# Load order, implied waits, idle matmuls, two copies and score groups: a change to the start of a fused attention and MLP kernel

## The chip, the cores and the metric

The kernel runs on one core of one Trainium2 chip. The metric is the device time of one execution in microseconds (us). Most executions of one kernel lie within about 1 us of each other, but not all, so each kernel is run several times; the span of a profile is some 1.8 us shorter than the time of the same execution, because it counts from the first to the last recorded instruction.

PE is the matmul engine and PEld its weight loads; DVE, ACT (ScalarE), POOL (GpSimd) and SP (SyncE) are the others. A DMA "lands" when its data is there.

## The reference

Attention with a window of 32 positions to each side, for 8 batches and 8 heads of 576 positions and 64 dimensions, and then an MLP with a squared ReLU over all 4608 tokens. Everything enters and leaves as 32-bit floats; the kernel computes in bf16 on PE.

```python
scores = (1 / np.sqrt(64)) * q @ k.transpose(0, 1, 3, 2)           # 8 x 8 x 576 x 576
mask = np.abs(pos[:, None] - pos[None, :]) <= 32
attn = softmax(np.where(mask, scores, -1e9))
x = (attn @ v).transpose(0, 2, 1, 3).reshape(4608, 512)
h = x @ w_in                                                       # 512 x 2048
r = np.maximum(h, 0.0)
out = (r * r) @ w_out                                              # 2048 x 512
```

## The kernel before

The program is written as a list of operations. Each has an engine, what it reads and writes, a planned duration and, for a DMA, planned figures of its queue. A list scheduler orders them: it runs a model forward and backward several times and keeps the order that does best over random repetitions of the model. So a change of one constant can reorder work anywhere.

The early loads go to GpSimd's queue in a written order. `w10` is the first quarter of `w_in`'s columns, `v04` the fifth and last V piece of batch 0:

```python
SIZES = (3,) * 9 + (4,) * 9        # groups of score steps of 64 tokens from batch 1 on
ORDER = ("k01 q01 v00 v01 v02 k03 q03 v03 k04 q04 w10 v04 w11 w12 w13 k05 q05 k10 q10 v10 k11 q11 v11 "
         "w20 w21 w22 w23 k12 q12 v12 k13 q13 v13 k14 q14 v14").split()
```

After scheduling, gaps in PE's plan up to the first MLP tile get idle matmuls, which multiply zeros so that PE's clock stays up:

```python
def fill(self, out):
    at = 1200                                              # ns of the plan
    for op in sorted((o for o in out if o.eng == "PE"), key=lambda o: o.start):
        gap = min(op.start, WARM, self.first.start) - at
        one = 107 if at < COLD else 54
        for k in range(int((gap - 60) * (DENSE if at < COLD else SPARSE) // one)
                       + (EXTRA if op is self.first else 0)):
            ...                                            # one idle matmul of 128 columns
        at = max(at, op.start + op.dur)
```

Last, the waits are written. An engine that has already waited for a value of a semaphore doesn't wait for it again, but what the other engine had itself waited for isn't known:

```python
for s, v in need.items():
    if waited.get((op.eng, s), 0) >= v:
        continue
    waited[(op.eng, s)] = v
    e.wait_ge(sems[s] if s in sems else dsems[s], v)
```

The MLP begins with small tiles of 128 tokens (`mm1_small`, the first of which is "the first MLP tile" below), goes over to 256 and then to 512 tokens. A small tile needs the transposed attention output `xt` and a quarter of `w_in`:

```python
def mm1_small(self, T, g, q, key):                         # cut
    def f(e):
        for d in range(4 * q, 4 * q + 4):
            for ft in range(4):
                mm = e.matmul(ht[:, 128 * (d % 4):...], self.W1[:, ft, 128 * d:128 * d + 128],
                              self.XT[:, ft, t0:t0 + 128], start=(ft == 0), stop=(ft == 3))
        return mm
    first = self.p.rec("PE", f, reads=[("xt", 8 * T + 2 * g), ("xt", 8 * T + 2 * g + 1), ("w1", q)], ...)
```

From step 18 on, `xt` is made by transposing DMAs on SP; before that PE transposes `xr`, the attention output as it comes, and ScalarE copies the result.

The softmax here doesn't subtract the row's maximum and nothing guards it: scores larger than these inputs give would overflow.

## Time and profile before

| | before |
|---|---|
| time, median of the first 3 runs | 300.18 us (299.93 to 300.94) |
| span of the profile | 298.4 us |
| PE busy | 293.1 us, 98% |
| first MLP tile starts | 18.21 us |
| last matmul ends | 296.10 us |

The prediction below shows the lines that it reads. Two more views help to follow it. The page's list of costly groups (line, engine, operation, what it writes and reads, partitions x elements, count, then busy time and mean ns of one, then idle time before) says where PE's time goes, and the list of DMA queues (packets, MB, share of 16 engines' span) how full the loading queue is:

```profile
q0 software_dynamic: 113120, 17.90, 89.8%
...
L919 PE MATMUL outp<-w,gt 128*128 128x512 bf16 x560 | 134.5, 379 | 0.0
...
L867 PE MATMUL ht<-xt,w 128*128 128x512 bf16 x384 | 93.7, 379 | 0.3 <-issue 0.3
```

The two big matmul groups have next to no idle time before them, and the queue that loads inputs and weights is occupied for 90% of the span. The second view is PE's timeline at the start (start us, duration us, what, count). It shows whether the clock is up:

```profile
2.77 2.13 PE L416 MATMUL outp<-zz 128*128 128x128 bf16 x18
...
7.91 1.09 PE L495 MATMUL ht<-oe,pf 128*128 128x128 f32 x8
```

Eighteen idle matmuls of 128 columns take 2.13 us, start to start about 107 ns: cold. From 5.25 us on the same kind takes 56 ns: warm. Eight of the 14 traces also hold records of the granted clock, which `prof` prints only as means; that of before goes up at 5.03 us.

### The profile page before, as it was taken

The numbers are of one execution on the slowest core, as the hardware profiler recorded it, in microseconds if no ns is written. First come the engines' busy times: TensorE is split into PE (matmuls) and PEld (weight loads), VectorE is DVE, ScalarE is ACT, GpSimd is POOL, SyncE is SP. The second block draws the span as 40 slices with busy tenths as digits, with TensorE's granted clock in tenths as the row PEclk, the third lists the DMA queues.
The fourth block names the chain that finished last, engine by engine and source line by source line (L and its number), as shares of the span: only waits on it lengthen the run. The fifth ranks groups of instructions, "written<-read, shape, count | busy, mean of one in ns | idle before, by whom it ended". The sixth has DMA issues, their size and how long they took to land.

```text
span 298.4 us, 7058 instructions
## 1 busy us (share of the span) xinstructions
PE 293.1 (98%) x2789; PEld 172.0 (58%) x2789; DVE 175.7 (59%) x428; ACT 160.5 (54%) x261; POOL 105.2 (35%) x131
## 2 busy tenths in 40 slices
PE   7899999999999999999999999999999999999996
PEld 7799855867668754544444545544445544444445
DVE  5864755674979966866386666773827682322200
ACT  3466543656657654763555656636645565444411
POOL 8999841332425434351254353313520000000000
PEclk9999999999999999999999999999999999999999
DMA  9999999999999999999499999999992230000022
GB/s 153 166 202 170 206 174 194 174 162 165 187 176 131 133 156 149 159 131 187 63 138 153 173 139 171 117 140 148 126 174 81 64 82 9 35 35 35 36 88 90
DMA packets 166817, 39.34 MB, mean 132 GB/s; under 512 B 157824, under 2 KB 162304, under 8 KB 166784
## 3 DMA queue, kind: packets, MB, share of 16 engines
q0 software_dynamic: 113120, 17.90, 89.8%
q1 hardware_dynamic: 46512, 11.15, 25.2%
q10 hardware_dynamic: 7152, 9.83, 10.1%
q8 instruction: 22, 0.36, 0.5%
q14 instruction: 11, 0.09, 0.1%
HBM read 36.70 MB, written 9.44 MB: 155 GB/s over the span
## 4 chain that ended last, share of the span: by engine, by line
PE 95%; DMA 2%; DVE 2%; issue 0%; POOL 0%; POOLq 0%
PE outp L919 41%; PE ht L867 28%; PE ht L849 7%; PE ht L826 7%; PE sc L703 3%; PE sc L647 3%; DMA qraw<-in_q_dram 2%; PE sc L495 1%; DVE vd L547 1%; PE outp L416 1%; PE sc L895 1%; PE outp L895 1%; DVE xr L791 1%; PE ht L495 0%; PE sc L751 0%; PE outp L807 0%
## 5 line engine op out<-in xcount | busy, mean ns | idle before, releaser
L919 PE MATMUL outp<-w,gt 128*128 128x512 bf16 x560 | 134.5, 379 | 0.0
L882 DVE TENSOR_TENSOR gt<-rt 128x512 bf16<-128x512 bf16 x144 | 59.5, 420 | 62.2 <-ACT rt L873 53.6
L867 PE MATMUL ht<-xt,w 128*128 128x512 bf16 x384 | 93.7, 379 | 0.3 <-issue 0.3
L919 PEld LDWEIGHTS outp<-w,gt 128*128 128x128 bf16 x560 | 52.9, 98 | 58.9
L873 ACT ACTIVATE rt<-ht 128x512 bf16<-128x512 f32 x96 | 57.4, 598 | 51.4 <-PE ht L867 48.9
L867 PEld LDWEIGHTS ht<-xt,w 128*128 128x128 bf16 x384 | 36.3, 98 | 41.9 <-issue 0.4
L469 POOL DMA_DIRECT2D qraw<-in_q_dram x39 | 33.6, 863 | 57.4 <-PE ht L867 20.6
L469 POOL DMA_DIRECT2D kraw<-in_k_dram x39 | 33.6, 860 | 35.1 <-PE ht L867 17.2
L535 POOL DMA_DIRECT2D vx<-in_v_dram x40 | 34.6, 866 | 21.3 <-PE ht L867 13.3
L684 DVE TENSOR_TENSOR pt<-e,mask 128x512 bf16<-128x512 bf16 (+1 forms) x63 | 29.9, 508 | 19.9 <-ACT e L668 19.1
L926 ACT ACTIVATE oe<-outp 128x512 f32<-128x512 f32 x35 | 20.9, 597 | 35.0 <-PE outp L919 34.9
L668 ACT ACTIVATE e<-sc 128x1024 bf16<-128x1024 f32 (+1 forms) x36 | 31.8, 917 | 6.4 <-PE sc L647 6.3
L727 DVE TENSOR_TENSOR xr<-pf,rs 128x512 bf16<-128x512 f32 (+1 forms) x42 | 27.5, 682 | 0.4
L826 PE MATMUL ht<-xt,w 128*128 128x128 bf16 x384 | 23.8, 219 | 0.0
L849 PE MATMUL ht<-xt,w 128*128 128x256 bf16 x192 | 23.3, 273 | 0.0
L826 PEld LDWEIGHTS ht<-xt,w 128*128 128x128 bf16 x384 | 21.7, 98 | 0.3
L720 DVE COPY pf<-sc 128x520 f32<-128x520 f32 x21 | 14.6, 697 | 8.8 <-PE sc L703 8.6
L849 PEld LDWEIGHTS ht<-xt,w 128*128 128x128 bf16 x192 | 18.0, 98 | 3.1
L717 ACT ACTIVATE pf<-sc 128x520 f32<-128x520 f32 x21 | 12.6, 602 | 13.0 <-PE sc L703 11.4
L834 ACT ACTIVATE rt<-ht 128x512 bf16<-128x512 f32 x24 | 14.2, 599 | 9.1 <-PE ht L826 8.8
L855 ACT ACTIVATE rt<-ht 128x512 bf16<-128x512 f32 x24 | 14.3, 600 | 6.0 <-PE ht L849 4.3
L722 DVE TENSOR_TENSOR pf<-pf 64x520 f32<-64x520 f32 x21 | 14.6, 697 | 2.2 <-ACT pf L717 1.2
(83 smaller groups left out, 180.3 us busy)
## 6 DMA issues: line engine op xcount, KB each, us to landing
out_dram<-oe ACTq DMA_DIRECT2D x35, 256.0 KB, 2.9
kraw<-in_k_dram POOLq DMA_DIRECT2D x30, 128.0 KB, 5.7
qraw<-in_q_dram POOLq DMA_DIRECT2D x30, 128.0 KB, 5.9
vx<-in_v_dram POOLq DMA_DIRECT2D x24, 128.0 KB, 5.4
w<-in_moe_w_in_dram POOLq DMA_DIRECT2D x4, 512.0 KB, 10.2
w<-in_moe_w_out_dram POOLq DMA_DIRECT2D x4, 512.0 KB, 16.4
vx<-in_v_dram POOLq DMA_DIRECT2D x16, 96.0 KB, 5.3
xt<-xr SPq DMA_TRANSPOSE x36, 4.0
```

What stands on the lines that cost most here:

```text
L469: self.p.rec("POOL", lambda e: e.dma_start(dst, src), writes=[("fraw", b, t, x)], old=[("fraw", b - 2, t, y + (b == 2))], reads=self.pace( ...
L535: self.p.rec("POOL", lambda e: e.dma_start(self.VX[b % 2][r:r + n, s, :, 0:64], self.v[b, :, t0:t0 + n, :].rearrange("h p d -> p h d")), w ...
L668: self.p.rec("ACT", lambda e, d=dst, a=src: e.activation(d, a, ACTF.Exp, scale=0.125), reads=["s" + x for x in ("AC", "BD")[h]], writes=[( ...
L684: self.p.rec("DVE", lambda e: e.tensor_tensor(pt, ee, mb, ALU.mult), reads=[("e", g // 2)] + rd, writes=[("ptt", k)], old=old, key=key + k ...
L727: self.p.rec("DVE", lambda e, w=w, np=np: e.tensor_tensor(bass.AP(self.XR, 512 * (2 * y + w), [[2048, np], [64, 2], [128, 4], [1, 64]]), b ...
L826: mm = e.matmul(ht[:, 128 * (d % 4):128 * (d % 4) + 128], self.W1[:, ft, 128 * d:128 * d + 128], self.XT[:, ft, t0:t0 + 128], start=(ft == ...
L849: mm = e.matmul(ht[:, 256 * (d % 2):256 * (d % 2) + 256], self.W1[:, ft, 128 * d:128 * d + 128], self.XT[:, ft, 64 * s0:64 * s0 + 256], st ...
L867: mm = e.matmul(ht[:], self.W1[:, ft, 128 * d:128 * d + 128], self.XT[:, ft, 512 * T:512 * T + 512], start=(ft == 0), stop=(ft == 3))
L873: self.p.rec("ACT", lambda e: e.activation(rt[:], ht[:], ACTF.Relu), reads=[("ht", k % 2)], writes=[("rt", k % 4)], key=key, dur=560)
L882: self.p.rec("DVE", lambda e: e.tensor_tensor(g, r, r, ALU.mult), reads=[("rt", k % 4)], writes=tags, key=key, dur=430)
L919: mm = e.matmul(op, gt[:, d, 128 * u:128 * u + 128], self.W2[:, d, :], start=(d == 0), stop=(d == 15))
L926: self.p.rec("ACT", lambda e: e.activation(oe[:], op, ACTF.Copy), reads=[tag], writes=[("oe", x % 4)], key=key, dur=560)
```

## The change

It has five parts. The second weight quarter is issued ahead of the fifth V piece. Waits that another wait implies are dropped. There are fewer but wider idle matmuls, and they begin later. Two early V copies go from DVE to ScalarE. The score groups of four start later in the program. Small memsets are merged besides, 29 into 10. The intent is an earlier first MLP tile and fewer instructions. The diff, cut to its core:

```diff
-WARM, COLD, DENSE, SPARSE, EXTRA = 36000, 6000, 1.15, 0.95, 6
+FIRST, WARM, COLD, DENSE, SPARSE, LASTF = 4000, 36000, 6000, 1.15, 0.7, 0.4
-SIZES = (3,) * 9 + (4,) * 9
+SIZES = (3,) * 13 + (4,) * 6
+VDACT = ((0, 0), (2, 0))
-ORDER = ("k01 q01 v00 v01 v02 k03 q03 v03 k04 q04 w10 v04 w11 w12 w13 ...
+ORDER = ("k01 q01 v00 v01 v02 k03 q03 v03 k04 q04 w10 w11 v04 w12 w13 ...
     def fill(self, out):
-        at = 1200
+        at = FIRST
...
-            for k in range(int((gap - 60) * (DENSE if at < COLD else SPARSE) // one) + (EXTRA if op is self.first else 0)):
+            cols = max(0, int((gap - 60) * (DENSE if at < COLD else LASTF if op is self.first else SPARSE) / one * 4)) * 32
+            t = at
+            while cols >= 192:
+                n = min(cols, 512)
...
     def emit(self):
-            for s, v in need.items():
-                if waited.get((op.eng, s), 0) >= v:
+            seen = known[op.eng]
+            while need:
+                s = max(need, key=lambda s: (s in sems, sum(v <= at.get((s, need[s]), {}).get(x, 0) for x, v in need.items() if x != s)))
+                v = need.pop(s)
+                if seen.get(s, 0) >= v:
                     continue
-                waited[(op.eng, s)] = v
                 e.wait_ge(sems[s] if s in sems else dsems[s], v)
+                for x, y in at[(s, v)].items():
+                    seen[x] = max(seen.get(x, 0), y)
...
+            if not b and (s0, lo) in VDACT:
+                self.p.rec("ACT", lambda e, d=dst, c=src: e.activation(d, c, ACTF.Copy), ...)
...
-   writes=[("w1", d)], dma=(f"w1{d}", 0), key=key, dur=770, move=(32, 82 if d else 95, 500))
+   writes=[("w1", d)], dma=(f"w1{d}", 0), key=key, dur=770, move=(32, 82, 500 if d > 1 else 1300))
```

The last line changes only what the scheduler believes of the landing of the first two weight quarters.

More of the change, by code (lines that the diff above doesn't have):

```diff
@@ L35 @@
 DEPTH, POST, BACK = 4000, {"POOL": 1500, "SP": 1000, "ACT": 1000}, {"POOL": 2500, "SP": 4000, "ACT": 4000}
-ORDER = ("k01 q01 v00 v01 v02 k03 q03 v03 k04 q04 w10 v04 w11 w12 w13 k05 q05 k10 q10 v10 k11 q11 v11 "
+ORDER = ("k01 q01 v00 v01 v02 k03 q03 v03 k04 q04 w10 w11 v04 w12 w13 k05 q05 k10 q10 v10 k11 q11 v11 "
          "w20 w21 w22 w23 k12 q12 v12 k13 q13 v13 k14 q14 v14").split()
@@ L315, in fill @@
             one = 107 if at < COLD else 54
-            for k in range(int((gap - 60) * (DENSE if at < COLD else SPARSE) // one) + (EXTRA if op is self.first else 0)):
+            cols = max(0, int((gap - 60) * (DENSE if at < COLD else LASTF if op is self.first else SPARSE) / one * 4)) * 32
+            t = at
+            while cols >= 192:
                 w = Op()
-                w.eng, w.fn, w.dma, w.deps, w.i = "PE", self.idle, None, {self.idle_on}, op.i
-                w.inc, w.val, w.sem, w.start, w.end, w.dur, w.key = False, None, None, min(at + one * k, op.start - 1), 0, one, -99
+                n = min(cols, 512)
+                w.eng, w.fn, w.dma, w.deps, w.i = "PE", (lambda e, n=n: self.idle(e, n)), None, {self.idle_on}, op.i
+                w.inc, w.val, w.sem, w.start, w.end, w.dur, w.key = False, None, None, min(t, op.start - 1), 0, one * n // 128, -99
                 out.append(w)
+                t, cols = t + w.dur, cols - n
             at = max(at, op.start + op.dur)
@@ L336, in emit @@
                 total[op.dma] = dcount[op.dma[0]] = dcount.get(op.dma[0], 0) + 16
-        waited = {}
+        known = {e: {} for e in engs}
+        at = {}
         for op in self.ops:
@@ L355, in emit @@
                 op.sem, op.val = s, total[op.dma]
+                info = at.setdefault((s, op.val), {s: op.val})
+                for x, y in seen.items():
+                    info[x] = max(info.get(x, 0), y)
                 ins.then_inc(dsems[s], 16)
@@ L359, in emit @@
                 op.sem, op.val = op.eng, count[op.eng]
+                at[(op.sem, op.val)] = {**seen, op.eng: op.val}
                 ins.then_inc(sems[op.eng], 1)
@@ L415, in setup_idle @@
         self.p.idle_on = self.p.ops[-1]
-        self.p.idle = lambda e: e.matmul(self.OUTP[1][:, 0:128], self.ZZ[:, 0:128], self.ZZ[:, 0:128], start=True, stop=True)
+        self.p.idle = lambda e, n: e.matmul(self.OUTP[1][:, 0:n], self.ZZ[:, 0:128], bass.AP(self.ZZ, 0, [[128, 128], [0, n // 32], [1, 32]]),
+                                            start=True, stop=True)
     def setup_masks(self, key):
@@ L437, in setup_rest, with setup_ptz @@
     def setup_rest(self, i, key):
+        self.ms("DVE", [("vxone", i)], self.VX[i][:, :, :, 64:VS], 1.0, key, 130)
         for s, r in ((0, 0), (4, 96)):
-            self.ms("DVE", [("vxz", i, s)], self.VX[i][r:r + 32, s, :, :], 0.0, key, 160)
-        self.ms("DVE", [("vxone", i, 0)], self.VX[i][32:64, 0, :, 64:VS], 1.0, key, 80)
-        self.ms("DVE", [("vxone", i, 1)], self.VX[i][64:128, 0, :, 64:VS], 1.0, key, 80)
-        self.ms("DVE", [("vxone", i, 2)], self.VX[i][0:96, 4, :, 64:VS], 1.0, key, 80)
-        self.ms("DVE", [("vxone", i, 3)], self.VX[i][:, 1:4, :, 64:VS], 1.0, key, 120)
-        self.ms("DVE", [("ktpad", i, 0)], self.KT[i][:, :, 0:32], 0.0, key)
-        self.ms("DVE", [("ktpad", i, 1)], self.KT[i][:, :, 32 + S_:KW], 0.0, key)
-    def setup_ptz(self, i, key):
-        for j in range(4):
-            self.ms("DVE", [("ptz", i)], self.PT[:, 768 * i + 192 * j + 64:768 * i + 192 * j + 128], 0.0, key, 70)
+            self.p.rec("DVE", lambda e, s=s, r=r: e.memset(self.VX[i][r:r + 32, s, :, :], 0.0), reads=[("vxone", i)],
+                       writes=[("vxz", i, s)], key=key, dur=160)
+        self.ms("DVE", [("ktpad", i)], bass.AP(self.KT[i], 0, [[4 * KW, 128], [KW, 4], [32 + S_, 2], [1, 32]]), 0.0, key, 160)
+    def setup_ptz(self, key):
+        self.ms("DVE", ["ptz"], bass.AP(self.PT, 64, [[2304, 128], [192, 12], [1, 64]]), 0.0, key, 300)
     def pieces(self, b):
@@ L545, in vd_half @@
             src = vx[64 - 64 * lo:128 - 64 * lo, s0 + lo:s1 + lo, :, :].rearrange("p s h d -> p (s h d)")
-            rd = list(tie) + [("vxl", b % 2, s + lo) + u for s in range(s0, s1) for u in ((), (1,))] + [("vxone", b % 2, k) for k in range(4)]
-            self.p.rec("DVE", lambda e, d=dst, c=src: e.tensor_copy(d, c), reads=rd,
-                       writes=[("vd", b % 2, s, lo) for s in range(s0, s1)], key=key, dur=80 + 145 * (s1 - s0), att=True)
+            rd = list(tie) + [("vxl", b % 2, s + lo) + u for s in range(s0, s1) for u in ((), (1,))] + [("vxone", b % 2)]
+            to = [("vd", b % 2, s, lo) for s in range(s0, s1)]
+            if not b and (s0, lo) in VDACT:
+                self.p.rec("ACT", lambda e, d=dst, c=src: e.activation(d, c, ACTF.Copy), reads=rd, writes=to, key=key,
+                           dur=200 + 560 * (s1 - s0), att=True)
+            else:
+                self.p.rec("DVE", lambda e, d=dst, c=src: e.tensor_copy(d, c), reads=rd, writes=to, key=key,
+                           dur=80 + 145 * (s1 - s0) if b else 120 + 300 * (s1 - s0), att=True)
     def load_w1(self, d, key):
@@ L562, in qk_tags @@
         i = b % 2
-        rd = [("ktpad", i, 0), ("ktpad", i, 1)]
+        rd = [("ktpad", i)]
         for x, (t0, n) in enumerate(self.pieces(b)):
@@ L690, in v_tags @@
             return [("vd", i, s, 0), ("vd", i, s, 1)]
-        return [("vxl", i, s), ("vxl", i, s, 1)] + [("vxone", i, k) for k in range(4)] + ([("vxz", i, s)] if s in (0, 4) else [])
+        return [("vxl", i, s), ("vxl", i, s, 1)] + [("vxone", i)] + ([("vxz", i, s)] if s in (0, 4) else [])
     def av3(self, n, w):
@@ L780, in f @@
             return mm
-        self.p.rec("PE", f, reads=self.v_tags(b, c) + [("pt", x), ("ptz", x)], writes=[tag], key=key, dur=240, att=True)
+        self.p.rec("PE", f, reads=self.v_tags(b, c) + [("pt", x), "ptz"], writes=[tag], key=key, dur=240, att=True)
     def evac(self, n, m, gi, k):
@@ L977, in build @@
         self.setup_rest(0, K + 3)
-        self.setup_ptz(0, K + 2)
-        self.setup_ptz(1, K + 2)
-        self.setup_ptz(2, K + 2)
+        self.setup_ptz(K + 2)
         self.setup_rest(1, -20)
```

## The prediction

> **What bounds the kernel now.** I read the page first: busy shares, slices, then the chain that ended last. TensorE (PE) is busy 98% of the span and the chain lies on it for 95%.
>
> ```profile
> span 298.4 us, 7058 instructions
> PE 293.1 (98%) x2789; PEld 172.0 (58%) x2789; DVE 175.7 (59%) x428; ACT 160.5 (54%) x261; POOL 105.2 (35%) x131
> PE   7899999999999999999999999999999999999996
> PE 95%; DMA 2%; DVE 2%; issue 0%; POOL 0%; POOLq 0%
> ```
>
> Busy is not useful work here: early PE time holds idle matmuls (outp<-zz) that only keep its clock up. So I read the timeline of PE, and the granted clock (1.00 throughout), and looked for every place where one PE group does not start when the one before has streamed through. The places that matter:
>
> ```profile
> 17.32 1.05 PE L416 MATMUL outp<-zz 128*128 128x128 bf16 x16
> 18.21 1.06 PE L826 MATMUL ht<-xt,w 128*128 128x128 bf16 x16
> 19.10 0.39 PE L807 MATMUL outp<-identw,xr 128*128 128x128 bf16 x4
> ...
> 20.73 1.05 PE L826 MATMUL ht<-xt,w 128*128 128x128 bf16 x16
> 21.89 0.40 PE L807 MATMUL outp<-identw,xr 128*128 128x128 bf16 x4
> ...
> 111.21 0.41 PE L703 MATMUL sc<-vx,pt 128*128 128x65 bf16 x8
> 111.88 1.02 PE L867 MATMUL ht<-xt,w 128*128 128x512 bf16 x4 [0.27 <-issue]
> ```
>
> The first useful MLP matmul starts at 18.21. Sixteen of them, start to start, take 19.10 - 18.21 = 0.89 us (56 ns each). After 18.21 the PE hardly stops: 20.73 + 0.89 = 21.62 to 21.89 is one hole (0.27 us; the chain has DVE's xr there), and before 111.88 another of some 0.43 us (eight of 29 ns from 111.21 end at 111.45). I found no third of this size up to the end at 298.4. So the kernel has two parts: a start of 18.2 us in which the PE waits for data, and 280.2 us of PE work laid end to end. The second can hardly shrink: its matmuls are the same in both kernels.
>
> What sets 18.21? The view of the line that loads the first weight half, limited to its first quarter, and that of the transposed loads just before 111.88:
>
> ```profile
> L552 POOL DMA_DIRECT2D w<-in_moe_w_in_dram x1: 832/832/832, 9.7 to 9.7; - x1
> DMA to landing us min/median/max: 7.8/7.8/7.8
> L738 SPq DMA_TRANSPOSE xt<-xr x1: 1257/1257/1257, 105.2 to 105.2; - x1
> DMA to landing us min/median/max: 6.6/6.6/6.6
> ```
>
> Issued at 9.66, the quarter lands at 9.66 + 7.81 = 17.47. PE finished its attention work at 17.32, then ran 16 idle matmuls, statically placed, up to 18.21: some 0.7 us after the weights were there. The transpose issued at 105.15 lands at 111.79, so the hole at 111.88 is a late DMA, not the four waits of that matmul.
>
> **What the Trainium skill says.** (1) "TensorE: Matmul & The Clock Gate", Part 1: 106.7 ns start to start for 128 columns while cold, 55.6 ns warm, and about 3.4 us of sustained work to become warm, in a free-running window. The trace agrees: idle matmuls step by 107 ns until about 4.9 us, by 56 ns after 5.2, having begun at 0.99 (about 4 us). (2) "DMA: Bandwidth & Descriptors", Queues, rings and completion order: a ring's descriptors are taken in order. The trace agrees as far as GpSimd's loads land in order of issue: w10 17.48, fifth V piece 18.10, second quarter 20.60, third 23.14, fourth 25.74. (3) "TensorEngine Tiling (Array Packing)", Key Properties: changing the tiling mode drains the array. The 64-row score matmuls show it: a group of four steps starts at 119.99 where the matmul before (119.68 + 0.22) frees the array at 119.90, and the matmul after comes at 120.56; a group of three takes 97.54 to 98.00 and about 0.10 before.
>
> **The change part by part.**
>
> *Weights.* On GpSimd w11 changes places with the fifth V piece. That V piece held the queue for 18.10 - 17.48 = 0.62 us. So w10 stays at 17.48, w11 comes at 20.60 - 0.62 = 19.98, the V piece at 20.60; the later loads stay.
>
> *Idle matmuls.* 103 of 128 columns become 17 of up to 512, and they start at 4.0 us instead of 1.2. Ahead of the first MLP matmul stands one of 512 columns (0.22 us: the chain has 1.73 us for eight such) instead of 16 x 56 ns = 0.89.
>
> *V copies.* Two of DVE's early V copies (1.61 us for the first three, 0.69 for the next two: about 0.54 and 0.35 each) go to ScalarE, which idles there. DVE's chain to the first xr (12.33 + 0.42) gets up to 0.9 us shorter. PE order also changes: the transpose of the fourth q piece no longer stands behind the xr transpose that started at 12.81 after 0.94 us idle.
>
> *Waits.* Counting the waits in the two programs: PE 436 to 333, DVE 467 to 400, ScalarE 451 to 397, GpSimd 176 to 90, SyncE 155 to 100. An instruction takes one; more become extra instructions, about 260 of which go. On PE they cost nothing that I can find: score groups behind four, five and six waits have the same 0.10 us gap. GpSimd and SyncE are off the chain. I give this 0.
>
> *Score groups.* 9 threes and 9 fours become 13 threes and 6 fours: 19 instead of 18. By the stretches above a three costs 0.56 and a four 0.66, so 13 x 0.56 + 6 x 0.66 = 11.24 against 9 x 0.56 + 9 x 0.66 = 10.98: +0.26 us (calculated from rounded starts, about 0.2 from drain and refill alone).
>
> **The sum**, on PE with the order of the changed program. Attention work before the first MLP matmul ends at about 17.0 to 17.3; the one filler fits before 17.5; the first MLP tile starts at 17.54 instead of 18.21: **-0.67**. Then in the new order: tile to 18.43; transpose of the third pair, which needs xr: DVE must do the reciprocal, a mask (0.42) and xr (0.69) after the attention product ends near 17.1, so about 18.8, a new stall of 0.35; attention product to 19.3, tile to 20.2, tile with w11 (19.98, no stall) to 21.1; then the product that needs the V piece: lands 20.60, copy 0.40, plus semaphores, 21.14; it ends at 21.39. At the same set of work the kernel before stood at 21.62 and then lost 0.27. So the lead is 0.23, then 0.50. The next transposes come one tile earlier in the order, at 26.08, and their q piece lands at 14.21 + 11.95 = 26.17: about 0.14 lost, lead **0.36**. The last quarter of the second weight (before: landed at 22.11 + 19.17 = 41.28, used at 41.98) would cap any lead at 0.65, so it doesn't bite.
>
> The hole at 111.88: I added the PE work between the attention product that feeds the last columns of this tile and its first matmul. Before: 101.95 to 111.45, 9.5 us, and the data took 9.84. In the new order it is 1.1 us more, so the hole should close: **-0.4**. The next tile has 0.5 us less than before, 8.8 against 9.3; its data took 6.4 before (136.01 to 142.31). No stall unless its transpose is as slow as the slowest (6.7 us).
>
> Sum: -0.36 - 0.43 + 0.2 to 0.26 = about -0.55 us. I allow 0.1 to 0.2 more because a schedule with less on DVE may beat my hand placement at the start: **predicted 299.5 us**, 0.7 under 300.18.
>
> **The rivals.** (a) *The start shrinks more.* If the stall before the third transpose doesn't happen and the V copy is quick, the lead is the whole 0.67, close to the cap of 0.65 that w23 sets; with the hole gone, -0.9: 299.2. For it: ScalarE's help and the earlier q transpose. Against: w10's landing is a floor that no part moves.
> (b) *The PE stays cold.* With no idle work before 2.3 us and a pause until k's first piece lands (4.03), the sustained work begins at 4.1, so the clock may open only between 7.5 and 11. Then fillers laid out for 56 ns run at 107 and stand in the way: 1792 columns before the second attention product would take 1.5 us, not 0.75. Slack until 17.48 hides most; at worst the first tile starts near 18.5 and the time is 300.3 to 300.7. Against: the kernel before stayed warm with the PE under half busy from 6.2 to 9.
> (c) *A new hole later.* Reordered score groups change when V, K and xt are needed; DMA latency of the transposes varies from 2.3 to 6.7 us. One missed transpose costs 0.4 to 2 us: 300 to 301.5. For it: the margin of the next tile. Against: after 22 us only one wait was missed before, and other engines are near half idle (DVE 59%, ScalarE 54%).
> (d) *Implied waits cost PE time after all.* Some 50 fewer extra instructions on PE, if each took as long as a 128-column matmul (56 ns, a guess), would be 2.8 us: 297. Against: no gap in the trace grows with the number of waits.
>
> **Range and chances.** 2% is 6.0 us. Faster than 294.2 would need a third of the start removed while w10's landing stays; I give 1%. Slower than 306.2 would need several new holes of a size that this trace has nowhere; 1%. The rest, 98%, is within. The three times of before spread by 1.0 us, which is more than the effect I expect; with (a) at the low end and (b), (c) above, the range is 298.6 to 300.5.
>
> **What would show each step right or wrong** in the profile of the changed kernel: about 6600 instructions, PE matmuls 2789 - 86 = 2703; the first MLP tile at 17.5 to 17.7, preceded by one 512-column filler; a hole of about 0.35 us before the transpose behind it; w11 landing near 20.0 and the V piece near 20.6; the turn of the 32-token piece near 26.2; no hole before the fourth tile's first 512-column matmul; 19 score groups, 0.1 us ahead of each; about 278.5 us or a little less from the first tile to the end of the span. Cold steps of 107 ns after 7.5 us would mean rival (b). It would be wrong above all if w10 lands at another time, if the attention work ends after 17.5, or if a hole of over 0.5 us stands somewhere after 30 us. A span that falls by 2 us or more without an earlier first tile would mean that the waits did cost time.

## The result and the profile after

| | before | after |
|---|---|---|
| time, median (4 runs each) | 300.06 us (299.76 to 300.94) | 299.69 us (299.62 to 300.20) |
| ratio, 95% interval | | 0.9987 (0.9963 to 1.0011) |
| span of the profile | 298.4 us | 297.8 us |
| first MLP tile starts | 18.21 us | 17.84 us |
| first MLP tile to the end of the last matmul | 277.89 us | 277.68 us |

Here and below a ratio is that of the fast runs of both kernels, as the record gives it; it isn't quite the ratio of the quoted medians.

The page of the changed kernel, the lines that answer to those of before:

```profile
span 297.8 us, 6573 instructions
PE 289.7 (97%) x2667; PEld 167.4 (56%) x2703; DVE 174.5 (59%) x407; ACT 160.9 (54%) x265; POOL 105.5 (35%) x131
```

There are 2703 weight loads but 2667 matmuls: 36 matmul records are missing from this trace. Gaps of exactly 216 ns between 512-column matmuls are those, not stalls, and the lower PE share of busy time comes in part from them. PE's timeline, at the places of the prediction:

```profile
8.09 1.11 PE L506 MATMUL ht<-oe,pf 128*128 128x128 f32 x4
...
10.89 0.92 PE L430 MATMUL outp<-zz 128*128 128x512 bf16 x4
...
17.48 0.38 PE L430 MATMUL outp<-zz 128*128 128x512 bf16 x1
17.84 1.07 PE L842 MATMUL ht<-xt,w 128*128 128x128 bf16 x16
18.95 0.40 PE L823 MATMUL outp<-identw,xr 128*128 128x128 bf16 x4
...
26.40 0.25 PE L506 MATMUL sc<-identw,kraw 32*128 32x32 bf16 x4
...
110.04 1.46 PE L935 MATMUL outp<-w,gt 128*128 128x512 bf16 x6
111.33 1.03 PE L883 MATMUL ht<-xt,w 128*128 128x512 bf16 x4
```

Read it from the top. At 8.09 four 32-bit transposes take as long as eight did before, so PE is still cold there. At 17.48 stands the one idle matmul of 512 columns (0.22 us). The first tile starts at 17.84, though the idle matmul was through at 17.70. What ends that wait is in the view of the line that loads the weights, for its first quarter (duration of the issue in ns, first and last start; then issue to landing):

```profile
L568 POOL DMA_DIRECT2D w<-in_moe_w_in_dram x1: 831/831/831, 9.7 to 9.7; - x1
...
DMA to landing us min/median/max: 8.1/8.1/8.1
```

The quarter lands at 17.79, 0.31 us later than in the profile of before, where it had taken 7.8 us. The tile's sixteen matmuls end at 17.84 + 0.89 = 18.73, and the transpose after it waits to 18.95 for `xr`. DVE's timeline tells why:

```profile
17.68 0.21 DVE L805 RECIPROCAL rs<-sc 128x8 f32<-128x8 f32 x1 [0.51 <-PE sc L795]
17.86 0.43 DVE L643 TENSOR_TENSOR pt<-e,mask 128x512 bf16<-128x512 bf16 x1
18.21 0.68 DVE L807 TENSOR_TENSOR xr<-sc,rs 128x512 bf16<-128x512 f32 x1
```

DVE waits 0.51 us for the attention product, and the order has a mask between the reciprocal and `xr`. So the earlier tile meets a later `xr`.

**The balance of the two profiles.** At the first matmul of the output layer both kernels have done the same PE work since their first tile (256 small MLP matmuls and the same transposes, scores and products). Before it starts at 35.75; after at 35.63 by the records, but one missing record of 0.22 us stands ahead of it, so at about 35.42. The lead there is 0.33 us. The hole of 0.43 us that before had at 111.88 isn't there after: six matmuls from 110.04 are through at 110.04 + 6 x 0.216 = 111.34, and the tile starts at 111.33. That would make -0.76 us. The spans differ by 298.39 - 297.82 = 0.57, so about +0.19 us is spread over the rest.

### The profile page after: what moved, and what is told of

The parts are those of the page before. It is cut to its first block, busy times and chain, and to the rows that moved or that the text cites. A ratio compares the mean times of both kernels' runs of the same rounds, so it can differ in the third digit from the quotient of the medians.

```text
span 297.8 us, 6573 instructions
## 1 busy us (share of the span) xinstructions
PE 289.7 (97%) x2667; PEld 167.4 (56%) x2703; DVE 174.5 (59%) x407; ACT 160.9 (54%) x265; POOL 105.5 (35%) x131
## 4 chain that ended last, share of the span: by engine, by line
PE 91%; DMA 3%; DVE 2%; ACT 1%; issue 1%; SPq 1%
PE outp L935 40%; PE ht L883 28%; PE ht L842 7%; PE ht L865 3%; PE sc L719 3%; PE sc L663 3%; DMA qt<-qraw 2%; PE ht L506 1%; DMA oe<-in_k_dram 1%; PE sc L506 1%; SPq L539 1%; PE outp L430 1%; ACT e L636 1%; PE sc L617 1%; PE sc L911 1%
## 5 line engine op out<-in xcount | busy, mean ns | idle before, releaser
L935 PE MATMUL outp<-w,gt 128*128 128x512 bf16 x535 | 132.0, 379 | 1.6 <-issue 0.5
```

The source lines that it names most:

```text
L935: mm = e.matmul(op, gt[:, d, 128 * u:128 * u + 128], self.W2[:, d, :], start=(d == 0), stop=(d == 15))
```

## The experiments

The theory was that the start is held by landings of DMAs, so that what the engines gain there becomes waiting, and that the rest is PE work which no part shortens. Its rivals were that dropped waits are worth time; that the idle work, now later, leaves PE cold and costs time; that the score groups cost or gain more than estimated; and that the load order or the copies matter on their own. Each kernel ran beside runs of the kernel before on the same chip: 11, 11 and 9 of them in the three batches, with medians of 300.03, 300.18 and 300.37 us.

| kernel | runs | median us | ratio to before (95%) | first tile us | first tile to last matmul us |
|---|---|---|---|---|---|
| waits_only | 6 | 300.43 | 1.0006 (0.9988 to 1.0025) | 18.21 | 277.77 |
| fill_only | 6 | 300.74 | 1.0016 (0.9998 to 1.0033) | 17.46 | 279.59 |
| sizes_only | 6 | 301.12 | 1.0026 (1.0010 to 1.0041) | 19.23 | 277.85 |
| order_only | 5 | 301.60 | 1.0047 (1.0031 to 1.0062) | 19.62 | 277.81 |
| after_again | 6 | 300.20 | 0.9993 (0.9968 to 1.0018) | 18.86 | 277.56 |
| after_oldfill | 6 | 299.82 | 0.9981 (0.9959 to 1.0004) | 18.07 | 277.60 |
| after_oldsizes | 6 | 300.31 | 0.9998 (0.9971 to 1.0025) | 17.87 | 277.75 |
| after_1_15 | 6 | 311.59 | 1.0371 (1.0336 to 1.0406) | 17.46 | 291.36 |
| after_warm | 5 | 300.07 | 0.9980 (0.9967 to 0.9994) | 17.24 | 278.99 |
| warm_oldsizes | 5 | 300.00 | 0.9982 (0.9970 to 0.9995) | 17.36 | 278.13 |
| warm_oldorder | 5 | 299.75 | 0.9978 (0.9965 to 0.9990) | 17.57 | 278.13 |
| warm_novd | 5 | 299.71 | 0.9981 (0.9968 to 0.9993) | 17.60 | 277.92 |

The last two columns come from the one profiled run of each kernel. All gave correct results, and all but after_1_15 lie within 2% of before.

### waits_only: the kernel before with the new writing of waits

```diff
-            for s, v in need.items():
-                if waited.get((op.eng, s), 0) >= v:
+            while need:
+                s = max(need, key=...)      # the rest of this hunk as in the change
```

> The kernel before with only the new emission of waits; the order on PE is the same instruction for instruction. Theory A (waits are free on a PE that is never starved by its sequencer): within 0.1% of before (299.8 to 300.4 us), the first tile at 18.2 us within 0.2, the hole before the first 512-column tile still 0.3 to 0.6 us, some 260 instructions fewer. Rival B (each extra wait instruction costs PE about what a small matmul does): 1 to 3 us faster, and the stretch from the first tile to the end shorter by that.

PE does the same work in the same order as before. The page and PE's timeline:

```profile
span 298.3 us, 6773 instructions
PE 289.9 (97%) x2755; PEld 171.7 (58%) x2789; DVE 175.5 (59%) x428; ACT 160.7 (54%) x261; POOL 105.2 (35%) x131
```

```profile
21.38 1.05 PE L835 MATMUL ht<-xt,w 128*128 128x128 bf16 x16 [0.52 <-ACT rt L843]
...
111.98 0.81 PE L876 MATMUL ht<-xt,w 128*128 128x512 bf16 x3
```

The page counts 285 instructions fewer, but 34 of these are matmul records that are missing from this trace (2755 matmuls for 2789 weight loads). The waits themselves are 251 instructions fewer, 47 of them on PE, and the ratio is 1.0006. Dropping implied waits is worth nothing measurable. The two timeline lines teach something else. The order is that of before, yet the hole at 111.88 is gone (the first of the tile's four matmuls is one of the missing records, so the tile began 0.22 us before 111.98) and one of 0.68 us stands at 21.38 instead, where the second weight quarter landed at 21.25 rather than 20.60 (the label in brackets names another event). Holes of this size come and go between runs of one order.

### fill_only: the kernel before with the new idle matmuls

```diff
-WARM, COLD, DENSE, SPARSE, EXTRA = 36000, 6000, 1.15, 0.95, 6
+FIRST, WARM, COLD, DENSE, SPARSE, LASTF = 4000, 36000, 6000, 1.15, 0.7, 0.4
-        at = 1200
+        at = FIRST                          # and the loop and the idle matmul as in the change
```

> The kernel before with only the new idle matmuls; the order of all other PE work is the same. Theory A: the first tile starts when the first weight quarter has landed (17.5 to 17.9 us instead of 18.2), but with the old order of loads the second quarter lands at about 20.6, so that the third tile can't start before 20.7 as in the kernel before: the lead of 0.4 to 0.7 us shrinks to 0.1 or less there, and the time is within 0.1% of before. Rival B (the idle matmuls were the cost): 0.4 to 0.7 us faster in the span. Rival C (the PE is cold too long): steps of 107 ns until after 8 us and the first tile later than 18.2.

The order is again that of before. PE's timeline, and the view of the line that issues the transposing DMAs, for the one at 104.8:

```profile
17.46 1.05 PE L831 MATMUL ht<-xt,w 128*128 128x128 bf16 x16
20.53 0.66 PE L831 MATMUL ht<-xt,w 128*128 128x128 bf16 x9 [0.21 <-DMA w<-in_moe_w_in_dram]
...
113.04 0.81 PE L872 MATMUL ht<-xt,w 128*128 128x512 bf16 x3 [1.93 <-DMA xt<-xr]
```

```profile
L743 SPq DMA_TRANSPOSE xt<-xr x1: 1197/1197/1197, 104.8 to 104.8; - x1
...
DMA to landing us min/median/max: 8.0/8.0/8.0
```

The idle matmuls alone bring the first tile forward by 0.75 us, to 17.46, as w10 landed at 17.27 and one filler stood in the way instead of sixteen. Little of it survives: 0.38 us are lost at 20.53 to the second quarter, and 1.87 ahead of the tile at 113.04 to a transpose that took 8.0 us. (Its data landed at 112.77 and its first weights were loaded at 112.81; the record of its first matmul, 0.22 us ahead of 113.04, is missing.) The place is that of the hole at 111.88 in the kernel before. So that place is sensitive to a late transpose, and the hole of before was one draw out of 0, 0.43 and 1.87 us in three profiles of one PE order. The clock went up at 7.43 us in this profile and the attention work still ended at 17.25, no later than before; so here it is the holes that make the kernel, if anything, slower.

### sizes_only and order_only: one constant of the kernel before

```diff
-SIZES = (3,) * 9 + (4,) * 9
+SIZES = (3,) * 13 + (4,) * 6
```

> The kernel before with only 13 threes and 6 fours of score steps; the scheduler makes a new order of it. Theory A: one more score group costs 0.2 us, and the new order has 10.3 instead of 9.5 us of PE work between the attention product and the first 512-column tile that needs it, so the hole of 0.43 us there closes: net -0.2 us, first tile still at about 18.2. Rival B (score groups or DVE pressure bind elsewhere): a new hole of over 0.3 us after 30 us.

```diff
-... k04 q04 w10 v04 w11 w12 ...
+... k04 q04 w10 w11 v04 w12 ...             # and the planned landing of w10 and w11 as in the change
```

> The kernel before with only the second weight quarter loaded ahead of the fifth V piece. Theory A: the quarter lands at about 20.0 us and the V piece at 20.7, but the first tile still waits behind 16 or so idle matmuls, at 18.2; the gain at the start is 0.2 us at most; the new order (10.6 us of work) closes the hole before the first 512-column tile: -0.4; together 0.3 to 0.6 us faster. Rival B (the weight order is what matters): the first tile earlier and over 0.6 us faster.

Both came out slower than before, by 0.26% and 0.47%, where I had expected both to be faster; and in the profiles both lose it before the first tile. PE's timeline of order_only:

```profile
18.34 1.45 PE L416 MATMUL outp<-zz 128*128 128x128 bf16 x23
```

The scheduler made another start. Attention work ends at 18.34 in both, against 17.32 before, and then come 23 idle matmuls up to the first tile at 19.62 (16 in sizes_only, first tile at 19.23), though the first weight quarter had landed by 17.6 in both. From the first tile on, both need the same 277.8 us as before. Taken as tests of their part, these two runs fail: under a scheduler a part alone is a clean test only if the order of the rest stays. What sizes_only does show is that the other group sizes don't cost PE anything that can be seen after the start: 277.85 against 277.89 us, with holes in both.

### after_again: the changed kernel, unchanged, once more

> The changed kernel once more, as the yardstick of this batch. Theory A: ratio to before 0.997 to 1.000 again; the first tile 0.05 us after the first weight quarter lands (17.3 to 17.9 us, which varies by half a microsecond between runs of any of these kernels), a hole of about 0.2 us before the transpose that follows, no hole or one of under 0.5 us before the first 512-column tile. Rival (the profile of the changed kernel was a lucky one): a hole of 1 us or more there and a ratio above 1.

Six runs: 300.54, 300.75, 299.64, 299.85, 299.79, 300.75. They fall on two levels some 0.9 us apart. The profile fell on the upper one. The view of the weight line for the first quarter, and PE's timeline:

```profile
L568 POOL DMA_DIRECT2D w<-in_moe_w_in_dram x1: 842/842/842, 9.6 to 9.6; - x1
...
DMA to landing us min/median/max: 6.9/6.9/6.9
```

```profile
11.19 1.63 PE L430 MATMUL outp<-zz 128*128 128x512 bf16 x4
12.66 0.19 PE L794 MATMUL sc<-vd,pt 128*128 128x65 bf16 x1
...
18.64 0.38 PE L430 MATMUL outp<-zz 128*128 128x512 bf16 x1
18.86 1.06 PE L842 MATMUL ht<-xt,w 128*128 128x128 bf16 x16
```

The first weights were there at 16.50, the earliest of all profiles, and still the first tile starts at 18.86, a full 1.02 us later than in the other profile of the same program. The idle block of 1792 columns shows why. Here it holds PE from 11.19 to 12.66, 1.47 us or 0.82 ns a column: cold. In the other profile it held PE from 10.89 to 11.66, 0.77 us or 0.43 ns a column: warm, since about 10.4. The clock record of after_again says the same: it goes up at 12.65 us. The order is fixed, so the delay goes down PE's whole start: attention work ends at 18.64 instead of 17.48. This is the prediction's rival (b), though the clock opened still later than the "between 7.5 and 11" that it named.

### after_oldfill: the changed kernel with the idle matmuls of before

```diff
-FIRST, WARM, COLD, DENSE, SPARSE, LASTF = 4000, 36000, 6000, 1.15, 0.7, 0.4
+WARM, COLD, DENSE, SPARSE, EXTRA = 36000, 6000, 1.15, 0.95, 6     # and fill as before
```

> The changed kernel with the old idle matmuls back; the order of all other work is the changed kernel's. 18 of 56 ns stand behind the attention work that ends at 17.3 to 17.5, so the first tile starts at 18.3 to 18.5 whenever the weights land. Theory A: 0.5 to 0.7 us later there, of which the hole before the next transpose (0.2 us) is given back: 0.3 to 0.5 us slower than the changed kernel, so about equal to before. Rival (the start doesn't matter, as later waits swallow its lead): equal to the changed kernel within 0.1 us.

Useful PE work stands in the order of the changed kernel. I had expected 0.3 to 0.5 us more; it came out no slower (299.82, and five of six runs between 299.69 and 299.94). The clock is up by 5.17 us and attention work ends at 17.07, but eighteen idle matmuls then hold the first tile to 18.07. My reading is that the two effects cancel: what the fewer fillers of the change win in front of the first tile, the late clock takes back in the runs in which it opens last.

### after_oldsizes and after_1_15: other score groups in the changed kernel

```diff
-SIZES = (3,) * 13 + (4,) * 6
+SIZES = (3,) * 9 + (4,) * 9
```

> The changed kernel with 9 threes and 9 fours. Its start is the changed kernel's, instruction for instruction. Theory A: one score group fewer is worth 0.2 us; 10.6 us of work ahead of the first 512-column tile, 8.4 us ahead of the second: 0.2 us faster than the changed kernel unless the second tile's data take over 8.4 us. Rival (fours early cost more than the drain, because they hold up the attention of the next tile): 0.3 us slower or more, with a hole before the second or third 512-column tile.

The old sizes give 0.9998 in the batch in which the change gives 0.9993. The two levels are there again (299.71, 299.75, 299.88 and 300.75, 300.76, 300.77). A cost or gain of 0.2 us by one group more cannot be told from this.

```diff
-SIZES = (3,) * 13 + (4,) * 6
+SIZES = (3,) * 1 + (4,) * 15
```

> The changed kernel with one three and 15 fours: 16 score groups instead of 19, same start. By the drain alone 0.6 us faster. But only 8.3 us of PE work stand between the attention product and the first 512-column tile, where the data took 9.8 us before and 10.2 us in the changed kernel: Theory A expects a hole of 1.5 to 2.5 us there, so 1 to 2 us slower than the changed kernel. Rival (group count is what counts): 0.6 us faster.

This has three groups fewer. The time is 11 us longer, where I had expected 1 to 2. The waits of PE between 45 and 100 us (who waits, for whom: total us, times, longest):

```profile
PE ht L842 <- DMA qraw<-in_q_dram: 2.6, 1, 2.6
PE ht L865 <- DMA xt<-xr: 1.8, 1, 1.8
```

Holes start at 54 us. PE is idle for 8.4 us between 45 and 130 us, and by the trace's clock record the clock falls to half twice, from 58.7 to 65.5 and from 92.8 to 96.2 us. Each fall comes after 3.41 us in which PE was busy for only 0.87 or 1.60 us, with no single gap over 2.6 us. The slow matmuls in these stretches are an estimated 4.3 us more, from their columns at the cold and the warm step. So groups of four early in the program starve the middle: the data that they need isn't there. The direction was as expected, the size and the place were not. Whether the position of the fours or the order that the scheduler then chose does it, I did not separate.

### The four kernels with early idle matmuls

after_warm is the changed kernel with idle matmuls from the time of before on; the other three undo one more part each.

```diff
-FIRST, WARM, COLD, DENSE, SPARSE, LASTF = 4000, 36000, 6000, 1.15, 0.7, 0.4
+FIRST, WARM, COLD, DENSE, SPARSE, LASTF = 1200, 36000, 6000, 1.15, 0.7, 0.4
```

> The changed kernel with one number changed: its idle matmuls may start at 1.2 us as in the kernel before, not at 4.0. Order of all other work as in the changed kernel. Theory A (the clock): the changed kernel begins cold and its clock opens[...]; when late, the first tile starts at 18.9 and the run takes 300.5 to 300.8 us, else 299.6 to 299.9. Here the clock opens by 6 us in every run: attention work done at 17.0 to 17.3, first tile at 17.4 to 17.9, all runs below 300.0 (299.4 to 299.9), ratio about 0.998. Rival (the two levels have another cause, such as DMA): still some runs at 300.5 to 300.8.

PE's timeline of its profile, which fell on the slowest of its five runs:

```profile
7.86 0.66 PE L506 MATMUL ht<-oe,pf 128*128 128x128 f32 x4
...
16.33 0.38 PE L430 MATMUL outp<-zz 128*128 128x512 bf16 x1
17.24 1.07 PE L842 MATMUL ht<-xt,w 128*128 128x128 bf16 x16 [0.53 <-DMA w<-in_moe_w_in_dram]
...
26.29 0.25 PE L506 MATMUL sc<-identw,kraw 32*128 32x32 bf16 x4 [0.38 <-DMA qraw<-in_q_dram]
```

Four transposes in 0.66 us: warm. Attention work is over at 16.33, about 1.1 us earlier than in the changed kernel's profile. The tile starts only 0.60 earlier, because it now waits for the weights, landed at 17.19. By 26.29, where the last q piece landed at 26.15, the lead over the changed kernel is down to 0.11 us. This is the theory in one fence: the engines' gain ends at the next landing. That this run still took 300.36 us has a later reason: another hole, of some 0.7 us, stands at 85.75, where a transposing DMA was late. I had expected all runs of after_warm below 300.0; three of the five were not.

```diff
 FIRST = 1200
-SIZES = (3,) * 13 + (4,) * 6
+SIZES = (3,) * 9 + (4,) * 9
```

> The same, and 9 threes and 9 fours again. Theory A: no runs at 300.5 to 300.8; 0.2 us less for one score group fewer, against a hole of about 0.4 us at 72 us that this order had in its profile with the cold start: equal to the kernel with early idle matmuls within 0.3 us. Rival (later fours are worth something): over 0.4 us slower than it.

```diff
 FIRST = 1200
-... w10 w11 v04 w12 ...
+... w10 v04 w11 w12 ...                     # and the planned landing of before
```

> The changed kernel with early idle matmuls and the old order of loads; the scheduler makes a new order of the work. Theory A: the second quarter lands at 20.4 to 20.7 instead of 19.9 to 20.1, so the tile that needs it has a hole, and the start loses 0.2 to 0.4 us against the kernel with early idle matmuls alone; everything later is within 0.2 us. Rival (the load order is worth nothing as the V piece is then the late one): equal within 0.1 us.

```diff
 FIRST = 1200
-VDACT = ((0, 0), (2, 0))
+VDACT = ()
```

> The changed kernel with early idle matmuls and all early V copies on DVE. Theory A: two copies of 0.3 to 0.55 us come back to DVE ahead of the first xr, so the attention work ends up to 0.5 us later, 17.3 to 17.8, which the landing of the first weight quarter mostly hides: 0 to 0.3 us slower than with early idle matmuls alone. Rival (ScalarE takes longer for a copy, 0.63 against 0.3 us, and that loses time): faster by 0.1 us or more.

None of the three differs from after_warm by more than these runs scatter: 0.9982, 0.9978 and 0.9981 against 0.9980. For warm_oldorder I had expected 0.2 to 0.4 us more than after_warm; it has the lowest ratio of the four. It does pay for the late quarter (a hole of 0.72 us at 20.79, w11 landed at 20.66), but it ends no later. So with the other parts in place, the group sizes, the load order and the copies are each worth less than the scatter. The copies do move the start: attention work ends at 17.40 in warm_novd's profile and at 16.33 in after_warm's, but the first tiles are only 0.36 us apart, since w10 landed at 17.25 and 17.19.

All four intervals lie below 1, by about 0.2% of the time, so these do beat the kernel before (all four against the same nine runs of it). That they beat the changed kernel isn't shown: they ran in another batch and the intervals overlap. What can be said is the share of bad runs. Of the 16 runs of the changed kernel and after_oldsizes, six took over 300.4 us; of the 26 runs of after_oldfill and the four kernels here, none did. Six of the 26 ran in the same batch as the bad ones, the others on another chip. One profile ties a bad run to the late clock; and the late clock can't be the only source of slow runs, since the kernel before, whose idle matmuls begin early, had runs of 301.22 and 302.20 in that batch.

## Why the prediction was right, and where its steps were not

The time (299.69 against 299.5) and the class were right, and the sum too: about -0.55 us for a span that is 0.57 shorter. The 0.1 to 0.2 us allowed besides did not come. Part of this is luck: with the six runs of after_again the median of the changed kernel is 299.82, and three of its ten runs lie above the predicted range. Point by point:

**The floor at the start.** Right in kind. The landing of w10 was taken as fixed at 17.47; over the profiles it lies between 17.2 and 17.8 in most, with 16.50 once. So the lead at the first tile was mis-sized: -0.37 measured for -0.67 predicted, of which 0.31 is that landing. The same order in after_again gives +0.65 instead, by the clock. The attention work was to end at 17.0 to 17.3 and ended at 17.48, behind a clock that opened late; the landing hid that. (The prediction cites the skill for the order in a ring. The page says this of the queues of SP and ACT, and adds that data may finish out of order; that GpSimd's loads land in order is what these traces show.)

**The stalls behind it.** The stall for `xr` was there: 0.21 us for 0.35, smaller because the tile was later. The product that needs the V piece was to end at 21.39 and ended at 21.46. The turn of the last q piece came at 26.40, with its data at 26.26, for 26.17 predicted; some 0.15 us were lost, for 0.14. The lead after all this was 0.33 us, for 0.36. The smaller first lead and the smaller stalls nearly cancel, since both end at the same later landings.

**The hole at 111.88.** It closed, for -0.43 us, but hardly by the step that the prediction gave. The view of the line that issues this transpose, in the changed kernel:

```profile
L754 SPq DMA_TRANSPOSE xt<-xr x1: 1269/1269/1269, 105.0 to 105.0; - x1
DMA to landing us min/median/max: 5.9/5.9/5.9
```

The PE work from the attention product to the tile grew by 1.1 us, as predicted (100.73 to 111.33, 10.6 us). But the transpose was issued 4.24 us after the product instead of 3.20 (`xr` was ready at 104.19, but SP was still issuing another transpose until 104.92), so nearly all of this was used up. What closed the hole is that the transpose then took 5.9 us and not 6.6 (landed at 110.88). With the 6.64 us of before, an estimate from these numbers leaves a hole of some 0.3 us. That the data would take about as long as before was the step that failed, and that the hole closed was in good part luck. In the PE order of before this hole was 0.43, 0 and 1.87 us in three profiles. The 0.43 us is therefore part of the balance of these two profiles and not a secure gain of the change.

**Waits at no cost.** Right: 251 fewer wait instructions in an unchanged PE order, ratio 1.0006. Rival (d) falls.

**The score groups.** +0.2 to 0.26 us predicted; the remainder of the balance is +0.19, but no run isolates it, and the timed runs with both sizes don't resolve it. It stays an estimate.

**The count.** 2703 matmuls are borne out by the weight loads, and by the page of after_again, which has 2703 of each. The statement of "about 278.5 us" from the first tile to the end of the span was a slip: it doesn't fit the prediction's own sum, and both kernels need some 280 us (297.82 - 17.84 = 279.98 after, 298.39 - 18.21 = 280.18 before).

**The rivals.** Rival (b), a cold PE, was set aside with the argument that before had stayed warm with PE half busy. That argument failed: staying warm is not becoming warm. It also misread the trace, in which PE was busy for 2.11 of the 2.80 us from 6.2 to 9, not under half. Both profiles of the changed kernel show cold steps well after 7.5 us. In one of them slack hid it, as the rival said; in the other the first tile came at 18.86 and the time was 300.54, for "near 18.5" and "300.3 to 300.7". The kernel's upper level of runs, up to 300.75, reaches past the predicted range, while the median lies well inside it. Rival (c) didn't appear in the changed kernel, but did in fill_only. Rival (a) did not come: the stall before the third transpose was there, and w10 landed later, not earlier.

**Left open.** Why the landing of w10 varies between 16.50 and 17.8 us, and that a transpose issued at about 105 us took 6.6 us in one profile and 8.0 in another; why the kernel before has runs of up to 302.20; what the load order and the copies are worth below 0.2%; and what of after_1_15's 11 us is due to the scheduler's choice.

## What to carry to other kernels

Where the start of a kernel is held by a row of landings, count a gain on an engine only up to the next landing, and check with a second profile whether that landing stays put. Idle matmuls have two prices, the time that they stand in the way and the time at which the clock opens; early ones in gaps cost nothing that could be seen here, late ones in front of the first tile held it up by 0.75 us in one profile, of which little reached the end. Under a scheduler, a part of a change tried alone is evidence only when the order of the rest is unchanged.

## What the Trainium skill lacked or had wrong

- "TensorE: Matmul & The Clock Gate", Part 1, has a free-running window of about 3.4 us, and the warm state after one busy window. The clock records agree with the window: in after_1_15 the clock changes at 7.50, 58.70, 65.52, 92.83 and 96.24 us, whole multiples of 3.41 us apart. The opening at about 10.4 us in the changed kernel's first profile fits it too: PE's steady work began at 4.06, and two windows later is 10.9, an estimate from the page's figure. What the page doesn't say is how full a window must be, and of what. In order_only the clock opened at 3.67, after 3.41 us in which PE was busy for 2.69, mostly with idle matmuls of 128 columns. In after_again it opened only at 12.65; the window before its last one (5.83 to 9.24, if the windows lie on the same grid) was busy for 3.29 of 3.41 us, with 32-bit transposes, 64-row scores and wide idle matmuls, and did not open it. With idle matmuls from the beginning the records have 3.67 to 6.17 us in five profiles; with the late ones they have 7.43, 7.50 and 12.65 in three.
- The same page's advice to leave the ramp out of models, as under 1% of the span, holds in size: the two levels of the changed kernel differ by 0.9 us, 0.3%. But that is more than twice the whole effect of this change.
- "DMA: Bandwidth & Descriptors" fits the time of one DMA by a fixed 2 us and its bytes, which for a 512 KB quarter would be an estimate of 3.2 us. Behind other loads, in a queue that is occupied for 90% of the span, the first quarter took 6.9 to 8.1 us in these runs, differing between two runs of one program by 1.2 us. The fit is for one DMA alone; the page gives no measure of the wait in a queue or of its variation.
- No page that I found gives the cost of extra waits in front of matmuls. The runs show none: 251 wait instructions fewer, 47 of them on PE, ratio 1.0006 (0.9988 to 1.0025).
